# A small mask filled in another step, block 0's weight splits issued in another order, a table held until block 0, and two pads

## The chip, the core and the metric

The kernel runs on one core of a Trainium2 chip. The core has TensorE for matmuls (PE in the profile), VectorE (DVE), ScalarE (ACT), GpSimd (POOL) and SyncE (SP), which issues most DMAs. Each engine serves its own instructions in order and waits for others by semaphores. The metric is the device time of one execution in microseconds (us), as the median of several.

## The reference

Attention, then a mixture of experts on its output, all in float32:

```python
# q, k, v: (8 batches, 8 heads, 576 tokens, 64)
mask_local = (rel >= 0) & (rel < 32)                    # heads 0 to 3
mask_strided = (rel >= 0) & (pos_k % 32 == pos_q % 32)  # heads 4 to 7
attn = softmax(where(mask, q @ k.T / 8, -1e9))          # rows divided by (sum + 1e-9)
x = (attn @ v) with heads side by side                  # (4608 tokens, 512)
logits = x @ w_gate + modality_bias[modality_id]        # 8 experts
e = argmax(logits); g = softmax(logits)[e]
out[token] = g * (relu(x @ w1[e]) @ w2[e])              # w1 512 x 1024, w2 1024 x 512
```

## The kernel before

**Attention** runs in 32 units (classes `Local` and `Strided`), each of which makes scores, a softmax, transposes and values. The order of TensorE is written by hand (`manual_schedule` around the loop over units); that of the other engines comes from the tile framework's scheduler. While units run, generators in `extra` are advanced by `pop`: for each of four pairs of batches (`bp` 0 to 3) they finish the tokens, compute the gate (`route`) and write each token into its expert's region of a buffer `xd` in HBM (`scatter`, indirect DMAs on GpSimd). `going` is a constant 0/1 mask for a scan in `route`.

**Blocks.** The expert layer works on blocks of 256 tokens of one expert, read from `xd`. `PHASES` says when their table is made: after pair 1 that of blocks 0 and 1, after pair 2 that of blocks 2 to 5, after pair 3 that of the rest (first five double blocks, two single ones and a half block). `slots(ph)` computes a table from the counts, with a matmul `ct` and, for blocks 2 to 5, 22 small operations on VectorE. Regions end in rows that nobody wrote; `empty` writes zeros (`in_nul`, 528 KB) over 256 rows of `xd`: once for `xd[0:256]`, and once behind each expert's last row (`blank`).

**One block** is `ffn`. For each of eight parts f of the hidden layer it splits the weights into a high and a low part (`wh` on ScalarE, `wl` on VectorE, in two halves of 512 columns), multiplies (`h`, 12 matmuls in `up`), evicts with relu into `hh` (ScalarE) and `hl` (VectorE), and multiplies again (`o`, 6 matmuls in `down`), two parts later (`LAG`). Its weights come in four tiles j of 1 MB, each for two parts: two tiles `raw`, and the two tiles `lqk` that attention used for queries. `load` fetches those of the next block when a tile is free; `gather` loads tokens (`fx`), `send` splits them into 16-bit halves (`rows`) and transposes them by DMA (`cols`), `split` makes `xh` and `xl`; `turn` does the same for block 0 on TensorE.

**Into block 0.** `early` issues the tokens and the weights of block 0, and the tokens of block 1, during the last units, at the places in `SPOTS`. Each of these is `paced`: it waits until the last matmul ahead of it in the program is done. `split_first` makes the `up` half of f 0 and 1 (`ws`) while attention still runs.

Of the kernel before, what the change touches and what calls it, by code (L numbers as in the profile page):

```python
# [11 lines left out]
F32 = mybir.dt.float32  # L12
# [4 lines left out]
AF = mybir.ActivationFunctionType  # L17
# [3 lines left out]
P = 128  # L21
# [10 lines left out]
PHASES = ((1, 2), (2, 4), (3, 20))  # L32
NDOUBLE, NSINGLE = 5, 2
ROW = DM + 16
# [20 lines left out]
}  # L55
LAG = 2
FIRST, SPLIT, SEND, GATHER, FAR = 1, 4, 6, 7, 6
BIG = -float(2 ** 30)


# [153 lines left out]
def attention_moe(ctx: ExitStack, tc: tile.TileContext, a, out):  # L214
    nc = tc.nc
# [32 lines left out]
    pin = tc.keep_in_program_order  # L248
# [4 lines left out]

    def modality():

        modf = cp.tile([P, 36], F32, name="modf")
        pin(nc.gpsimd.tensor_copy(modf[:], modi))
        nmod = cp.tile([P, 36], F32, name="nmod")
        pin(nc.gpsimd.tensor_scalar(nmod[:], modf[:], -1.0, 1.0, ALU.mult, ALU.add))
        bias0 = ap.tile([P, 36 * E], F32, tag="ls", bufs=1, name="bias0").rearrange("p (t e) -> p t e", e=E)  # L260

        def bc_e(t):
            return t.unsqueeze(2).to_broadcast([P, 36, E])

# [9 lines left out]
    cnt = cp.tile([P, NBP + 1, E], BF16, name="cnt")  # L274
    nc.vector.memset(cnt[:, 0, :], 0.0)
    going = cp.tile([P, E, 9], BF16, name="going")
    nc.vector.memset(going[:], 1.0)
    nc.vector.memset(going[:, :, 0], 0.0)

    written = []  # L280

# [5 lines left out]
    def paced(ins):  # L287

        behind(ins, next(i for i in reversed(nc.cur_bb.bb.instructions) if i.engine == mybir.EngineType.PE).name)
# [23 lines left out]
        tc.add_to_no_dep_group(f"gath{bp}", ins.ins)  # L313

    outs = _Group(tc, "outs")


    ap_cm = tc.tile_pool(name="ap", bufs=1)
# [523 lines left out]

    def empty(rows):
        ins = nc.sync.dma_start(rows, a["nul"])
        for q in range(NBP):
            tc.declare_no_dep(ins.ins, group=f"scat{q}", reason="distinct rows")
            tc.declare_no_dep(ins.ins, group=f"gath{q}", reason="distinct rows")
        tc.declare_no_dep(ins.ins, group="empty", reason="distinct rows")
        tc.add_to_no_dep_group("empty", ins.ins)
        written.append((NBP - 1, ins.ins.name))  # L850

    def first_token(ph, s):
        return nc.values_load(
            tables[ph][0][0:1, s:s + 1], engines=[mybir.EngineType.SP], min_val=0, max_val=E * REG + NT,
            skip_runtime_bounds_check_because="a block's first row of its expert's region")

    def token_rows(dst, rows, bp):
        ins = nc.sync.dma_start(dst, rows)
        if bp < NBP - 1:
            tc.declare_no_dep(ins.ins, group="empty", reason="distinct rows")  # L860
        collected(ins, bp)
        return ins
# [168 lines left out]
            nc.scalar.copy(xh[:, c, q], xs[:, c, :])  # L1031
            nc.vector.tensor_tensor(xl[:, c, q], xs[:, c, :], xh[:, c, q].bitcast(F32), ALU.subtract)  # L1032

    def ffn(fp, n, xh, xl, les, between, load=None):
        os = []
        w = SLOT * len(les)

        def up(f, wh, wl):
            hp = pa(f"h{n}{f}")[:, 0:w]
            k = 0  # L1040
            for c in range(4):
                a1 = slice(P * c, P * c + P)
                for wx, x in ((wh, xh), (wh, xl), (wl, xh)):
                    nc.tensor.matmul(hp, wx[:, a1], x[:, c, :], start=(k == 0), stop=(k == 11))  # L1044
                    k += 1
            if len(les) == 2:
                h2 = ap.tile([P, 2, w], F32R, tag=f"xc{2 + f % 2}", bufs=2, name=f"h2{n}{f}")
                hh, hl = h2[:, 0], h2[:, 1]
            else:
                hh = fp.tile([P, w], F32R, tag="hh", bufs=4, name=f"hh{n}{f}")  # L1050
                hl = fp.tile([P, w], F32R, tag="hl", bufs=4, name=f"hl{n}{f}")
            nc.scalar.activation(hh[:], hp, AF.Relu)  # L1052
            nc.vector.scalar_tensor_tensor(hl[:], hp, 0.0, hh.bitcast(F32), ALU.max, ALU.subtract)  # L1053
            return hh, hl

        def down(f, wh, wl, hh, hl):
            if f == 0:
                os.extend(pa(f"o{n}{h}") for h in range(2 * len(les)))
            for h in range(2 * len(les)):
                m = slice(P * h, P * h + P)  # L1060
                for i, (hx, w) in enumerate(((hh, wh), (hh, wl), (hl, wh))):
                    nc.tensor.matmul(os[h], hx[:, m], w[:, 512:1024],  # L1062
                                     start=(f == 0 and i == 0), stop=(f == 7 and i == 2))

        def finish():
            for h in range(2 * len(les)):
                le = les[h // 2][:, h % 2, :]
                y = fp.tile([P, DM], F32, tag="y", bufs=3, name=f"y{n}{h}")
                nc.scalar.mul(y[:], os[h], le[:, 1:2].bitcast(F32))  # L1069
                outs.add(nc.gpsimd.indirect_dma_start(  # L1070
                    out, IOA(ap=le[:, 0:1], axis=0), y[:], None, bounds_check=NT - 1, oob_is_err=False))

        def down_last(*args):
            down(*args)
            finish()

        for f in range(8):
            raw = raws[f // 2][:, f % 2, :]
            wh = fp.tile([P, 1024], F32R, tag="wh", bufs=5, name=f"wh{n}{f}")
            wl = fp.tile([P, 1024], F32R, tag="wl", bufs=5, name=f"wl{n}{f}")  # L1080
            up_w = ready.pop(f, None)
            for c0 in range(512 if up_w else 0, 1024, 512):
                c = slice(c0, c0 + 512)
                nc.scalar.copy(wh[:, c], raw[:, c])  # L1084
                nc.vector.tensor_tensor(wl[:, c], raw[:, c], wh[:, c].bitcast(F32), ALU.subtract)  # L1085
            if load and f % 2:
                load(f // 2)
            late.append(partial(down_last if f == 7 else down, f, wh, wl, *up(f, *(up_w or (wh, wl)))))
            between(f)
            settle(LAG)  # L1090

# [15 lines left out]

    tables = {}

    def after(bp, xt, xcs):  # L1110
        yield from finish_pair(bp, xt, xcs)
        yield
        for ph, (last_bp, _) in enumerate(PHASES):
            if bp == last_bp:
                yield from slots(ph)
                if ph == 0:
                    yield
                    calm.append(early())

    def early():  # L1120
        for j in range(2):
            n, t, sl = plan[j]
            xt = gathered[j, 0] = pre.tile([P, 2, ROW], F32, tag="fx", name=f"fx{n}0")
            at = first_token(t, sl[0])
            for h in range(2):
                paced(token_rows(xt[:, h, :], xd[bass.ds(at + P * h, P), :], PHASES[t][0]))
                yield
            for part in range(2):
                paced(expert_weights(0, 0, j, part))
                yield  # L1130
        for j in (2, 3):
            paced(expert_weights(0, 0, j))
            yield

    extra, calm = [], []

# [11 lines left out]
    def pop(k):  # L1148
        for _ in range(k):
            while extra and next(extra[0], extra) is extra:  # L1150
                extra.pop(0)
# [20 lines left out]
        return len(plan[k][2]) if k < len(plan) else 1  # L1172

    def gather(k, part=0):
        if k == len(plan):
            gathered[k, 0] = half_tokens()
        if k < len(plan) and part < parts(k):
            n, t, s = plan[k]
            gathered[k, part] = tokens(f"{n}{part}", t, s[part])
# [65 lines left out]
    man.__exit__(None, None, None)  # L1245
    lp_cm.__exit__(None, None, None)

    fp_cm = tc.tile_pool(name="fp", bufs=2, reuse_waits="tile")
    fp = fp_cm.__enter__()
    empty(xd[0:SLOT, :])  # L1250
    while 1 not in tables:
        pop(1)
    gather(2)
    for k, (n, *_) in enumerate(plan):
        def between(f):
            if k == 0 and f == FIRST:
                send(1, 0)
            if f == SPLIT:
                if k + 1 == len(plan):
                    turn(k + 1)  # L1260
                split(k + 1, 0)
            if f == SPLIT - 1 + parts(k + 1):
                split(k + 1, 1)
            if f == SEND:
                send(k + 2, 0)
            if f == GATHER:
                gather(k + 3, 0)
                send(k + 2, 1)
                gather(k + 3, 1)
            pop(POPF[k > 0])  # L1270
            if blanks:
                blanks.pop(0)()

        ffn(fp, n, *turned[k], between, partial(load, k + 1))

    half_ffn(fp, *turned[len(plan)])

# [40 lines left out]
```

## Time and profile before

| | |
|---|---|
| median of 3 runs | 583.71 us (583.25 to 584.79) |
| profiled execution | 579.87 us, its span 577.7, mean granted clock 0.994 |
| TensorE busy | 546.1 us (95% of the span) |
| VectorE, ScalarE, GpSimd busy | 375.9, 313.3, 90.2 us |
| DMA | 137.27 MB, mean 238 GB/s |

In the order of the page: attention takes the first 140 us, block 0 starts at 140, and from there TensorE does the `h` and `o` matmuls of the blocks one after the other. "Idle before <- releaser" in a row says how long the engine had nothing to do ahead of it, and which event ended that.

### The profile page before, as it was taken

What the parts mean: (1) busy time and instruction counts of PE and PEld (TensorE: products, weight loads), DVE (VectorE), ACT (ScalarE), POOL (GpSimd) and SP (SyncE); (2) the same over time, 40 slices, a digit from 0 to 9 for tenths busy, and PEclk for the clock granted to TensorE, in tenths of its full rate; (3) what the DMA queues carried; (4) which work ended last, traced back from release to release, by engine and by line L of the source; (5) the groups of instructions that cost most, each with busy time, mean ns of one, the idle gap of its engine ahead of it and who ended that gap; (6) DMA issues with size and microseconds to landing.
All of it is one profiled execution on the core that took longest, in us unless ns stands there. A gap on an engine that the chain in (4) does not pass through costs nothing.

```text
span 577.7 us, 13484 instructions
## 1 busy us (share of the span) xinstructions
PE 546.1 (95%) x5273; PEld 460.9 (80%) x5273; DVE 375.9 (65%) x942; ACT 313.3 (54%) x651; POOL 90.2 (16%) x106
## 2 busy tenths in 40 slices
PE   6889898898799999999999999999999999999995
PEld 3678677777689999899878888888888888889994
DVE  6887879788586996687765635635734634547541
ACT  3577777767666665566634353344343353356641
POOL 1020321225105311011010020020020020021320
PEclk9999999999899999999999999999999999999998
DMA  8999998979799999999985662572582543555621
GB/s 268 326 321 328 311 301 282 372 257 368 245 367 295 304 387 291 349 322 245 346 231 209 133 251 82 155 276 73 151 233 91 157 172 111 146 201 173 245 94 37
DMA packets 66087, 137.27 MB, mean 238 GB/s; under 512 B 40400, under 2 KB 40784, under 8 KB 58961
## 3 DMA queue, kind: packets, MB, share of 16 engines
q1 hardware_dynamic: 59312, 112.73, 61.3%
q0 software_dynamic: 6416, 23.37, 10.8%
q8 instruction: 43, 0.70, 0.5%
q10 hardware_dynamic: 288, 0.24, 0.1%
q14 instruction: 28, 0.22, 0.1%
HBM read 108.24 MB, written 24.30 MB: 229 GB/s over the span
## 4 chain that ended last, share of the span: by engine, by line
PE 76%; DMA 9%; DVE 6%; issue 4%; ACT 3%; SPq 1%; POOL 0%; POOLq 0%; DVEq 0%; ACTq 0%
PE o L1062 31%; PE h L1044 31%; DMA lqk<-in_w 5%; PE o L437 2%; PE s L389 2%; PE lg L610 1%; DMA cols<-rows 1%; PE oa L533 1%; PE xs L235 1%; DMA raw<-in_w 1%; PE ss L483 1%; PE xl L235 1%; PE t L235 1%; DVE wl L1085 1%; DMA lqk<-in_qkl 1%
## 5 line engine op out<-in xcount | busy, mean ns | idle before, releaser
L1044 PE MATMUL h<-xh,wl 128*128 128x256 f32 (+1 forms) x408 | 133.7, 328 | 0.5 <-DVE wl L1085 0.5
L1044 PE MATMUL h<-xl,wh 128*128 128x256 f32 (+1 forms) x408 | 133.5, 328 | 0.3 <-DVE xl L1032 0.3
L1044 PE MATMUL h<-xh,wh 128*128 128x256 f32 (+1 forms) x408 | 133.5, 328 | 0.0
L1062 PE MATMUL o<-wh,h 128*128 128x512 f32 x320 | 107.0, 396 | 0.0
L1085 DVE TENSOR_TENSOR wl<-lqk,wh 128x512 fp32r<-128x512 f32 x104 | 67.8, 687 | 56.4 <-ACT wh L1084 54.3
L1084 ACT CAST wh<-raw 128x512 fp32r<-128x512 f32 x102 | 58.5, 618 | 65.0 <-PE o L1062 59.7
L1085 DVE TENSOR_TENSOR wl<-raw,wh 128x512 fp32r<-128x512 f32 x102 | 66.4, 686 | 39.3 <-ACT wh L1084 39.2
L1070 POOL DMA_INDIRECT out<-y,le x36 | 40.7, 1130 | 306.3 <-ACT y L1069 299.7
L1084 ACT CAST wh<-lqk 128x512 fp32r<-128x512 f32 x104 | 59.7, 618 | 51.9 <-PE o L1062 49.2
L1044 PEld LDWEIGHTS h<-xl,wh 128*128 128x128 f32 x408 | 77.9, 191 | 10.2 <-DVE xl L1032 0.7
L1044 PEld LDWEIGHTS h<-xh,wh 128*128 128x128 f32 x408 | 77.7, 191 | 9.7
L1044 PEld LDWEIGHTS h<-xh,wl 128*128 128x128 f32 x408 | 77.9, 191 | 8.1 <-DVE wl L1085 0.8
L1062 PEld LDWEIGHTS o<-wh,h 128*128 128x128 f32 x320 | 60.1, 188 | 14.5
L1062 PE MATMUL o<-wl,h 128*128 128x512 f32 x160 | 63.3, 396 | 0.0
L1053 DVE SCALAR_TENSOR_TENSOR h<-h,h 128x512 fp32r<-128x512 f32 x40 | 27.6, 691 | 47.8 <-ACT h L1052 47.8
L1062 PE MATMUL o<-wh,hh 128*128 128x512 f32 x128 | 51.4, 402 | 3.5 <-ACT hh L1052 3.5
L1052 ACT ACTIVATE h<-h 128x512 fp32r<-128x512 f32 x40 | 23.9, 599 | 51.9 <-PE h L1044 51.7
L1062 PE MATMUL o<-wl,hh 128*128 128x512 f32 x128 | 50.6, 395 | 0.0
L1062 PE MATMUL o<-wh,hl 128*128 128x512 f32 x128 | 49.8, 393 | 0.0
L1062 PEld LDWEIGHTS o<-wl,h 128*128 128x128 f32 x160 | 30.0, 188 | 7.1
L1052 ACT ACTIVATE hh<-h 128x256 fp32r<-128x256 f32 x64 | 24.5, 385 | 17.9 <-PE h L1044 17.9
L678 POOL DMA_INDIRECT xd<-xa,posi x20 | 20.7, 1036 | 83.6 <-PE o L1062 30.7
(211 smaller groups left out, 837.8 us busy)
## 6 DMA issues: line engine op xcount, KB each, us to landing
lqk<-in_w SPq DMA_DIRECT2D x26, 1024.0 KB
raw<-in_w SPq DMA_DIRECT2D x24, 1024.0 KB
lqk<-in_qkl SPq DMA_DIRECT2D x32, 296.0 KB
vv<-in_vl SPq DMA_DIRECT2D x32, 292.5 KB
sqk<-in_qks SPq DMA_DIRECT2D x32, 288.0 KB
fx<-xd SPq DMA_DIRECT2D x16, 528.0 KB
vs<-in_vs SPq DMA_DIRECT2D x16, 320.0 KB
xd<-in_nul SPq DMA_DIRECT2D x9, 528.0 KB
```

What stands on the lines that cost most here:

```text
L235: nc.tensor.transpose(dst, src, ident)
L389: nc.tensor.matmul(sp[32 * u:32 * u + 32, 128 * m:128 * m + 128], q[:, i, :], kd[:, :, i:i + 2, :], start=False, stop=True, skip_group_che ...
L437: nc.tensor.matmul(o[64 * jj:64 * jj + 64, k, :], et[:, 2 * (k // 2) + bb, 2 * (k % 2) + jj, :, :].rearrange("p g q -> p (g q)"), vv[:, 4 ...
L483: nc.tensor.matmul(s[32 * u:32 * u + 18, 36 * i:36 * i + 36], qk[:, 32 + r, :], qk[:, r:r + 65:64, :], start=False, stop=True, skip_group_ ...
L678: ins = nc.gpsimd.indirect_dma_start(xd[:], IOA(ap=posi[:, i:i + 1], axis=0), x[:, j, :], None)
L1044: nc.tensor.matmul(hp, wx[:, a1], x[:, c, :], start=(k == 0), stop=(k == 11))
L1052: nc.scalar.activation(hh[:], hp, AF.Relu)
L1053: nc.vector.scalar_tensor_tensor(hl[:], hp, 0.0, hh.bitcast(F32), ALU.max, ALU.subtract)
L1062: nc.tensor.matmul(os[h], hx[:, m], w[:, 512:1024], start=(f == 0 and i == 0), stop=(f == 7 and i == 2))
L1070: outs.add(nc.gpsimd.indirect_dma_start(out, IOA(ap=le[:, 0:1], axis=0), y[:], None, bounds_check=NT - 1, oob_is_err=False))
L1084: nc.scalar.copy(wh[:, c], raw[:, c])
L1085: nc.vector.tensor_tensor(wl[:, c], raw[:, c], wh[:, c].bitcast(F32), ALU.subtract)
```

## The change

- The two memsets of `going` move from VectorE, at the program's start, to GpSimd in `modality`, which is called in unit 9's step.
- `cpad` (4864 bytes a partition) is allocated between the constants and the pool `ap`, `apad` (32 bytes) at the end of `ap`. Neither is read or written.
- `empty` is paced. The write of `xd[0:256]`, which stood first in SP's queue, now stands behind block 0's last weights.
- In block 0 (`first=True`) the splits of f + 1 are issued a step ahead, and from f 2 on a `wh` copy is ordered behind the eviction `hh` of f - 2.
- The table of blocks 2 to 5 waits for `over`, which is set in block 0 at f 1; what waits for the table comes at f 3 (`SECOND`), the tokens of block 2 with it.
- `early` issues in this order: tile 0 of the weights, tokens of block 0, tile 1, tile 2, tokens of block 1, tile 3 (before: tokens of block 0, tile 0, tokens of block 1, tiles 1, 2, 3).
- The half block's tokens are loaded once and not twice.

```diff
+FIRST, SECOND, SPLIT, SEND, GATHER, FAR = 1, 3, 4, 6, 7, 6
+CPAD = 1216
     def modality():
+        pin(nc.gpsimd.memset(going[:], 1.0))
+        pin(nc.gpsimd.memset(going[:, :, 0], 0.0))
...
-    nc.vector.memset(going[:], 1.0)
-    nc.vector.memset(going[:, :, 0], 0.0)
...
+    cp.tile([P, CPAD], F32, name="cpad")
...
     def empty(rows):
         ins = nc.sync.dma_start(rows, a["nul"])
+        paced(ins)
...
+        def split_weights(f):
             raw = raws[f // 2][:, f % 2, :]
...
-                nc.scalar.copy(wh[:, c], raw[:, c])
+                ins = nc.scalar.copy(wh[:, c], raw[:, c])
+                if first and f > 1:
+                    follow(ins, evicted[f - 2])
                 nc.vector.tensor_tensor(wl[:, c], raw[:, c], wh[:, c].bitcast(F32), ALU.subtract)
+            ws[f] = wh, wl, up_w or (wh, wl)
+        for f in range(8):
+            for g in ((f, f + 1) if f == 0 else (f + 1,)) if first else (f,):
+                if g < 8:
+                    split_weights(g)
...
             if bp == last_bp:
+                while ph == 1 and not over:
+                    yield
                 yield from slots(ph)
...
     def early():
...
         for j in range(2):
             for part in range(2):
                 paced(expert_weights(0, 0, j, part))
                 yield
-        for j in (2, 3):
-            paced(expert_weights(0, 0, j))
+            if j == 0:
+                for h in range(2):
+                    paced(half(0, h))
+                    yield
+        paced(expert_weights(0, 0, 2))
+        yield
+        for h in range(2):
+            paced(half(1, h))
             yield
+        paced(expert_weights(0, 0, 3))
+        yield
...
-        if k == len(plan):
+        if k == len(plan) and part == 0:
             gathered[k, 0] = half_tokens()
...
+    ap.tile([P, 8], F32, name="apad")
     empty(xd[0:SLOT, :])
-    while 1 not in tables:
-        pop(1)
-    gather(2)
...
             if k == 0 and f == FIRST:
                 send(1, 0)
+                over.append(True)
+            if k == 0 and f == SECOND:
+                while 1 not in tables:
+                    pop(1)
+                gather(2)
...
-        ffn(fp, n, *turned[k], between, partial(load, k + 1))
+        ffn(fp, n, *turned[k], between, partial(load, k + 1), first=k == 0)
```

ScalarE before, at the start of block 0 (`wh_02` is the high half of block 0's weights for f 2; `xc` are copies for pair 3's tokens):

```order
L1084 CAST wh_00_3138<-raw_2802 128x512
L1084 CAST wh_01_3165<-raw_2802 128x512
L1084 CAST wh_02_3207<-raw_2982 128x512 x2
L1084 CAST wh_03_3250<-raw_2982 128x512 x2
L568 COPY xc_141<-xl_3159 128x512
L1084 CAST wh_04_3289<-lqk_84 128x512 x2
L568 COPY xc_141<-xl_3198 128x512
L568 COPY xc_141<-xl_3204 128x128
L1052 ACTIVATE hh_00_3155<-h_00_3142 128x256
L1052 ACTIVATE hh_01_3186<-h_01_3173 128x256
```

And after:

```order
L1094 CAST wh_00_3095<-raw_2759 128x512
L1094 CAST wh_01_3099<-raw_2759 128x512
L570 COPY xc_140<-xl_3195 128x512
L1060 ACTIVATE hh_00_3116<-h_00_3103 128x256
L1094 CAST wh_02_3120<-raw_2845 128x512 x2
L1060 ACTIVATE hh_01_3143<-h_01_3130 128x256
L1094 CAST wh_03_3201<-raw_2845 128x512 x2
L570 COPY xc_140<-xl_3224 128x512
L570 COPY xc_140<-xl_3230 128x128
L1060 ACTIVATE hh_02_3220<-h_02_3207 128x256
L1094 CAST wh_04_3241<-lqk_83 128x512 x2
```

The evictions `hh` move up between the copies `wh`; `wh_04`, the first that reads a tile `lqk`, moves from ahead of `hh_00` to behind `hh_02`.

VectorE before, in block 0 (`fx_10` and `rows_10` are tokens of block 1):

```order
L1085 TENSOR_TENSOR wl_00_3139<-raw_2802,wh_00_3138 128x512
L1085 TENSOR_TENSOR wl_01_3166<-raw_2802,wh_01_3165 128x512
L1085 TENSOR_TENSOR wl_02_3208<-raw_2982,wh_02_3207 128x512 x2
L1085 TENSOR_TENSOR wl_03_3251<-raw_2982,wh_03_3250 128x512 x2
L1085 TENSOR_TENSOR wl_04_3290<-lqk_84,wh_04_3289 128x512 x2
L1053 SCALAR_TENSOR_TENSOR hl_00_3156<-h_00_3142,hh_00_3155 128x256
L1053 SCALAR_TENSOR_TENSOR hl_01_3187<-h_01_3173,hh_01_3186 128x256
L1000 COPY rows_10_3190<-fx_10_2841 128x2x512 x2
L877 COPY le_10_3196<-fx_10_2841 128x8
L1053 SCALAR_TENSOR_TENSOR hl_02_3227<-h_02_3213,hh_02_3226 128x256
```

And after, from `hl_01` on (`off`, `ei`, `ge`, `tk`, `er`, `own` belong to the table of blocks 2 to 5):

```order
L1061 SCALAR_TENSOR_TENSOR hl_01_3144<-h_01_3130,hh_01_3143 128x256
L1003 COPY rows_10_3147<-fx_10_2972 128x2x512 x2
L880 COPY le_10_3153<-fx_10_2972 128x8
L769 TENSOR_TENSOR off_3166<-used_117,exc_3165 128x8
L787 TENSOR_REDUCE ei_3172<-gi_3170 128x4
L788 TENSOR_TENSOR ge_3171<-cf_sb,exc_3165 128x32
L831 TENSOR_SCALAR tk_3191<-exc_3165 128x8
L1097 TENSOR_TENSOR wl_03_3202<-raw_2845,wh_03_3201 128x512 x2
L806 TENSOR_SCALAR er_3182<-ei_3172 128x4
L789 TENSOR_TENSOR own_3157<-ge_3171,gi_3170 128x32
L832 SCALAR_TENSOR_TENSOR tk_3191<-tk_3191,nb_3162 128x8
L1061 SCALAR_TENSOR_TENSOR hl_02_3221<-h_02_3207,hh_02_3220 128x256
```

`rows_10` moves from behind `wl_04` to ahead of `wl_03`, and operations of the table stand between the splits.

SP after, from block 0's third tile on (names `lqk` hold tiles 2 and 3, `fx_10` the tokens of block 1; ISA rows compute addresses):

```order
L902 DMA lqk_83<-in_w 128x2048
L856 TENSOR_LOAD row_2167
L861 ISA
L861 DMA fx_10_2972<-xd 128x528
L861 ISA
L861 DMA fx_10_2972<-xd 128x528
L902 ISA
L902 DMA lqk_84<-in_w 128x2048
L846 DMA xd<-in_nul 16x8448
L891 TENSOR_LOAD eb_2172
L902 ISA
L902 DMA raw_2759<-in_w 128x2048
```

Tokens of block 1 stand between the third and the fourth tile, the write of zeros behind the fourth, and block 1's first weights follow it, ahead of the transposes of `rows_10`.

## Rows read from the trace of the kernel before

**Rows 1.** Waits of TensorE: for what, us in total, times, longest.
```profile
PE warm L345 <- DVE idle L341: 4.1, 1, 4.1
PE o L1062 <- ACT hh L1052: 3.5, 1, 3.5
...
PE ts L235 <- DVE bl L789: 1.3, 1, 1.3
```

**Rows 2.** Chain that ended last: start us, length us, what ran or landed.
```profile
133.73 14.17 DMA lqk<-in_w
...
151.33 2.56 PE h L1044 x12
156.60 1.43 PE h L1044 x12
```

**Rows 3.** Timeline, start: start us, us, engine, line, operation, [idle before <-releaser].
```profile
0.75 0.61 POOL L337 MEMSET lqk<- 128x608 f32 x1 [0.29 <-POOLq L1310]
...
0.75 0.67 SPq L844 DMA_DIRECT2D xd<-in_nul  x1
...
1.15 0.91 DVE L348 MEMSET et<- 128x1024 f32 x1 [0.16 <-issue]
...
2.35 0.58 POOL L342 MEMSET sqk<- 128x576 f32 x1
...
3.90 0.11 DVE L341 MEMSET idle<- 128x64 uint32 x1
...
8.32 1.08 PE L389 MATMUL s<-lqk 128*32 128x128 f32 x32
```

**Rows 4.** Windows: stretch, length us, busy us of five engines, PEclk, DMA share, GB/s.
```profile
4.00:12.00 8.00, 7.65 (x156) 4.34 (x159) 4.67 (x14) 1.02 (x3) 0.00 (x0) 1.00 0.94 316
125.50:127.50 2.00, 2.00 (x46) 1.74 (x46) 2.00 (x12) 1.43 (x5) 0.00 (x0) 1.00 0.31 75
140.00:147.00 7.00, 6.53 (x59) 6.25 (x55) 4.28 (x8) 4.88 (x9) 5.03 (x5) 1.00 1.03 423
147.00:154.00 7.00, 3.95 (x17) 3.73 (x18) 3.65 (x8) 3.67 (x10) 0.00 (x0) 0.79 0.61 237
154.00:161.00 7.00, 7.00 (x74) 5.39 (x74) 4.74 (x9) 4.97 (x11) 0.00 (x0) 0.97 0.84 240
161.00:168.00 7.00, 7.00 (x49) 6.43 (x48) 5.77 (x16) 5.07 (x12) 0.00 (x0) 1.00 1.02 424
224.00:231.00 7.00, 7.00 (x45) 6.31 (x45) 4.55 (x8) 3.99 (x8) 1.30 (x2) 1.00 1.10 216
237.00:560.00 323.00, 322.19 (x1591) 269.52 (x1590) 187.32 (x322) 155.10 (x283) 34.57 (x32) 1.00 0.61 193
```

**Rows 5.** Timeline, end of attention: SP's token load, TensorE's wait for vs.
```profile
126.03 0.96 SPq L858 DMA_DIRECT2D fx<-xd  x2
...
138.99 1.08 PE L533 MATMUL oa<-eb,vs 126*64 126x126 f32 x16 [1.36 <-DMA vs<-in_vs]
```

**Rows 6.** Timeline, block 0: ScalarE, VectorE and TensorE around the wait.
```profile
147.92 1.14 ACT L1084 CAST wh<-lqk 128x512 fp32r<-128x512 f32 x2 [1.94 <-DMA lqk<-in_w]
148.57 1.29 DVE L1085 TENSOR_TENSOR wl<-lqk,wh 128x512 fp32r<-128x512 f32 x2 [2.27 <-ACT wh L1084]
...
149.60 0.67 ACT L1052 ACTIVATE hh<-h 128x256 fp32r<-128x256 f32 x2
...
150.05 0.50 PE L1062 MATMUL o<-wh,hh 128*128 128x512 f32 x1 [3.52 <-ACT hh L1052]
...
150.70 1.28 DVE L1000 COPY rows<-fx 128x1024 uint16<-128x1024 uint16 x2
...
151.13 0.41 PE L1044 MATMUL h<-xh,wh 128*128 128x256 f32 x1
```

**Rows 7.** Timeline, start of block 4: its tokens on VectorE, TensorE's wait.
```profile
235.87 1.40 DVE L1017 COPY xs<-cols 128x1024 uint16<-128x1024 uint16 x2 [3.98 <-DMA cols<-rows]
...
237.88 0.39 PE L1044 MATMUL h<-xh,wl 128*128 128x256 f32 x1 [0.55 <-DVE wl L1085]
```

More of the change, by code (lines that the diff above doesn't have):

```diff
@@ L56 @@
 LAG = 2
-FIRST, SPLIT, SEND, GATHER, FAR = 1, 4, 6, 7, 6
+FIRST, SECOND, SPLIT, SEND, GATHER, FAR = 1, 3, 4, 6, 7, 6
+CPAD = 1216
 BIG = -float(2 ** 30)
@@ L1032, in split_tokens, with follow, ffn @@
             nc.vector.tensor_tensor(xl[:, c, q], xs[:, c, :], xh[:, c, q].bitcast(F32), ALU.subtract)
-    def ffn(fp, n, xh, xl, les, between, load=None):
-        os = []
+    def follow(ins, other):
+        tc.add_manual_dep(
+            ins.ins, other.ins.name,
+            mybir.DependencyInfo(mybir.DependencyClass.NoSync, mybir.DependencyReason.DATA), reason="order")
+    def ffn(fp, n, xh, xl, les, between, load=None, first=False):
+        os, evicted = [], {}
         w = SLOT * len(les)
@@ L1051, in up @@
                 hl = fp.tile([P, w], F32R, tag="hl", bufs=4, name=f"hl{n}{f}")
-            nc.scalar.activation(hh[:], hp, AF.Relu)
+            evicted[f] = nc.scalar.activation(hh[:], hp, AF.Relu)
             nc.vector.scalar_tensor_tensor(hl[:], hp, 0.0, hh.bitcast(F32), ALU.max, ALU.subtract)
@@ L1075, in down_last @@
             finish()
-        for f in range(8):
+        ws = {}
+        def split_weights(f):
             raw = raws[f // 2][:, f % 2, :]
@@ L1083, in ffn @@
                 c = slice(c0, c0 + 512)
-                nc.scalar.copy(wh[:, c], raw[:, c])
+                ins = nc.scalar.copy(wh[:, c], raw[:, c])
+                if first and f > 1:
+                    follow(ins, evicted[f - 2])
                 nc.vector.tensor_tensor(wl[:, c], raw[:, c], wh[:, c].bitcast(F32), ALU.subtract)
+            ws[f] = wh, wl, up_w or (wh, wl)
[3 more added lines that the diff above has]
+                    split_weights(g)
+            wh, wl, up_w = ws.pop(f)
             if load and f % 2:
                 load(f // 2)
-            late.append(partial(down_last if f == 7 else down, f, wh, wl, *up(f, *(up_w or (wh, wl)))))
+            late.append(partial(down_last if f == 7 else down, f, wh, wl, *up(f, *up_w)))
             between(f)
@@ L1108, in attention_moe @@
     tables = {}
+    over = []
     def after(bp, xt, xcs):
@@ L1120, in early, with half @@
     def early():
-        for j in range(2):
[L1122 to L1127, printed above, removed]
+        firsts = [first_token(plan[j][1], plan[j][2][0]) for j in range(2)]
+        def half(j, h):
+            n, t, _ = plan[j]
+            if h == 0:
+                gathered[j, 0] = pre.tile([P, 2, ROW], F32, tag="fx", name=f"fx{n}0")
+            return token_rows(gathered[j, 0][:, h, :], xd[bass.ds(firsts[j] + P * h, P), :], PHASES[t][0])
+        for j in range(2):
             for part in range(2):
```

## The prediction

> **What bounds the kernel now.** I read four views: TensorE's waits, the chain of what ended last, the timeline around the three places that the change touches, and the windows with the DMA share. TensorE has few waits, and the largest are where the change acts [rows 1]: 4.1 us at the start for the memset of `idle`, 1.3 us at the end of attention for the table of blocks 2 to 5, 3.5 us in block 0 for the eviction `hh`; the 1.4 us for `vs` between them is in [rows 5]. The chain [rows 2] names what stands behind the 3.5: the load of block 0's third weight tile (`lqk`), and the twelve matmuls after it take 2.56 us where twelve later ones take 1.43. Later TensorE runs back to back (busy 322.19 of the 323 us from 237 to 560 [rows 4]). So the time is the sum of matmuls plus these waits, and what is gained before block 1 stays gained unless the DMA stream cannot follow.
>
> Durations come from the profiled execution, 579.87 us (span 577.7); the median of the three timed runs is 583.71, 3.84 more. I sum on 579.87 and carry the 3.84 over.
>
> **1. The start: -1.8 us.** Before, the memset of `idle` starts at 3.90 on VectorE, the warm-up matmuls follow it and the first scores come at 8.32 [rows 3]. Ahead of `idle` stand two `et` memsets of 0.91 us each, which now come later: 2 x 0.91 = 1.8; the smaller ones that leave its front (`going`, `e`) I leave uncounted on the safe side. `idle` so ends near 2.1, the warm-up follows, and the first scores start near 6.5. They also need their load: the write of zeros to `xd` (528 KB), first in SP's queue at 0.75 [rows 3], no longer stands ahead of it. The next limit is the stream of query loads (share 0.94 from 4 to 12 us [rows 4]); it loses the 528 KB ahead of it, about 1.3 us at the 423 GB/s of a later full stretch [rows 4], so a part of the 1.8 could stay there. Bounds: 0 (the loads hold everything) to -2.4 (the small memsets too). I take 1.8, since TensorE, not the loads, was last at 8.32. The two `going` memsets cost nothing on POOL: its memsets at the start end at 2.93, and the mask is first used much later.
>
> In the rows POOL's memset of `lqk` runs from 0.75 to 1.36 and VectorE's `et` from 1.15 to 2.06, side by side, at the same rate per element (0.61 us for 608, 0.91 us for 1024) [rows 3]. The Trainium skill says otherwise for some pairs (SBUF — State Buffer, section SBUF: two separate sides): the port pair that VectorE and GpSimd share is an exclusive lock, and the later one blocks for a whole instruction. [...]
>
> **2. End of attention: -0.8 us.** The 22 small VectorE operations of the table leave this stretch; one of them, `bl`, is what the wait of 1.3 us is put down to [rows 1]. But a little later TensorE waits 1.36 us for `vs` at 138.99 [rows 5], so what comes earlier before it is swallowed there unless `vs` lands earlier. Ahead of `vs` now stands another weight half in place of one token half (512 against 264 KB: +0.25 MB, 0.6 us at 423 GB/s); on the other side SP held the token loads until 126.03, while the stream had a share of only 0.31 from 125.5 to 127.5 [rows 4, 5], and weights, which need no tokens, now fill it: 0.69 x 2 = 1.4 us. So `vs` is 1.4 - 0.6 = 0.8 us earlier. Bounds: +0.6 (the gap isn't filled) to -2.7 (both waits go).
>
> **3. Block 0: -1.6 us.** Before, ScalarE's queue has `wh` f4 (`wh_04`) ahead of `hh_00`; `wh_04` waits for its weights until 147.92, and TensorE's `o` starts at 150.05 after 3.52 us of nothing [rows 6]. After, `hh_00` stands ahead of `wh_02`, and so on alternately. The wait that takes its place is for `wh_02`: after `h_00` ScalarE runs one eviction (two take 0.67, one 0.33) and half a weight copy (1.14 / 2 = 0.57) [rows 6]; together 0.9, if none of it lies beside `h_01`: 3.5 - 0.9 = 2.6. The second half of the copies and the subtractions lie beside the matmuls, which take 1.43 us per f [rows 2].
>
> A new wait on VectorE: `rows_10` waits for `fx1`, which now comes behind the third weight tile, and `wl_03`, the table and `hl_02` queue behind it. `lqk` of the third tile was there at 147.92; 0.5 MB of `fx1` now comes after it and not before it, so the third tile lands earlier and `fx1` at about where the tile was, less the filled gap: 147.9 - 1.4 = 146.5. Two `rows` copies (1.28), the five small operations behind them (some 0.5 by the 0.1 that each holds the queue, an estimate) and half of a `wl` pair (0.65) [rows 6] bring 148.9. TensorE needs `wl_03` in the third matmul of the `h` that started at 151.13 [rows 6] before: 2.6 and the 0.8 of term 2 earlier, and two matmuls later, that is 147.9. So it waits 1.0 there, and term 3 is -2.6 + 1.0 = -1.6. Bounds: 0 (the wait grows to the gain) to -3.5.
>
> **4. The clock: -1.7 us.** Behind the 3.5 us of idle the granted clock is 0.79 from 147 to 154 and 0.97 from 154 to 161 [rows 4]: 0.21 x 7 + 0.03 x 7 = 1.7 us, which is 1.2 GHz for some 3.4 us. Waits of 0.9 and 1.0 are shorter than the 1.3 and 1.4 before it [rows 1, 5], behind which the clock was 1.00 from 140 to 147 [rows 4], so the whole of it comes back. Bounds 0 to -1.7.
>
> **5. Given back at block 4: +0.7 us.** Up to here TensorE is 1.8 + 0.8 + 1.6 + 1.7 = 5.9 us early. From 161 us on the stream is full (share 1.02, 424 GB/s; 1.10 from 224 to 231 [rows 4]), and at 235.87 block 4's tokens come just in time: TensorE waits 0.55 at 237.88 [rows 7]. What the stream can gain: it starts 1.8 + 0.8 = 2.6 earlier; from 147 to 161 it has 0.39 x 7 + 0.16 x 7 = 3.8 us of room, into which block 1's first weights now go (they no longer wait behind the transposes of `cols_10`); and it has the zeros to carry that left the start, +1.4 with their share of the queue. 2.6 + 3.8 - 1.4 = 5.0, so it is 5.9 - 5.0 = 0.9 behind TensorE. The share is under 1 in places after that too, so I take 0.7. Bounds: 0 to +4.7 (no room: 5.9 - 2.6 + 1.4).
>
> That stream rate speaks against a page: the Trainium skill (DMA: Bandwidth & Descriptors, section Where 436 GB/s comes from) lets the HBM side bind at about 358 GB/s for such loads. By it the 161 to 168 stretch could not carry what it did (424, [rows 4]), so the trace disagrees, and the full rate is used above.
>
> **6. Nothing:** the two pads move addresses alone (no row shows a duration that hangs on an address; bounds -1 to +1); the dropped second load of the half block's tokens (264 KB) lies late, where the stream has room; the pacing of the eight zero writes waits on matmuls that are long past.
>
> **The sum:** -1.8 - 0.8 - 1.6 - 1.7 + 0.7 = -5.2: 574.7 profiled, 578.5 as a median.
>
> **Rivals.** A, the forecast: 578.5, its own range 575.5 to 581.5.
>
> B, the stream has no room: block 4 comes 1.2 us earlier (2.6 - 1.4) whatever TensorE does; TensorE waits 4.7 us there and runs its first microseconds at 1.2 GHz, 1.7 more. -1.2 + 1.7 = +0.5: 584.2. For it speaks the share of about 1 from 161 on; against it the 3.8 us of room before that, and that loads ahead of 200 us are released by TensorE's progress.
>
> C, the start gives nothing: VectorE's first memsets wait behind POOL's, which end at 2.93 (2.35 + 0.58) [rows 3], so that `lqk` and `idle` on VectorE end at about 3.6 against 4.0, and the loads hold what is left. The sum without the 1.8: 578.5 + 1.8 = 580.3. Against it: the two engines' memsets side by side.
>
> D, slower: VectorE is held by `rows_10` for `fx1` far longer than the 1.0 of term 3. TensorE idles y = (landing of `fx1`) - 145.5, since 146.5 gives 1.0, and falls to 1.2 GHz behind it, so that term 4 is lost and nothing is given back: -1.8 - 0.8 - 2.6 + y = y - 5.2. It is slower than before from y = 5.2, a landing at 150.7, and tells itself from no change from y = 7; with a landing at 154.5 y is 9: +3.8, 587.5. For it: the slow end of the load of the third tile, and that VectorE serves its queue in order. Against it: `fx1` stands before the fourth tile and the zeros in the queue, and its half tiles are a quarter of a weight tile.
>
> **Numbers.** A 0.58, B 0.16, C 0.13, D 0.13. A measurement of this kernel tells 0.3% from no change, which is 1.75 us: faster is under 581.96, slower above 585.46. A and C are faster (0.71, and a little of B's near side: 0.72); B's middle and D up to y = 7 lie within (0.19); D beyond that and B's far end are slower (0.09). The range 574.5 to 583.8 holds A, C, the near half of B and the first part of D; it leaves out some 0.2.
>
> **What would show it.** The wait for `idle` near 2 us; the wait of `o` for `hh` gone and one under 1 us for `wh` or `wl` in its place; granted clock 1.00 from 147 to 161; `vs` earlier; a wait of some 1 us for `wl_03` behind `rows_10`; at block 4 a wait of `h` for `xs`, `cols` or `wl` of about 1 us, and back to back after it. Wrong if block 4's wait is above 4 us (B), if the first scores stay at 8.3 (C), or if VectorE's wait for `fx` leaves TensorE idle behind `wl_03` for over 3 us (D).

## The result, and the profile after

| | before | after |
|---|---|---|
| median | 583.48 us (4 runs, 580.3 to 584.79) | 576.77 us (4 runs, 573.91 to 577.81) |
| ratio of the medians, 95% interval | | 0.9891 [0.9849, 0.9934] |
| profiled execution, its span, clock | 579.87, 577.7, 0.994 | 577.81, 575.7, 0.987 |

The change makes the kernel 6.7 us faster; 5.2 were forecast. The two profiles differ by only 2.06 us, since the profiled execution of before lies 3.6 us under its median and that of after 1.0 over its own. So the two traces have to be compared by stage. TensorE's first `h` of block 0 is the border: 140.13 us before, 145.71 after. The windows below have the columns of [rows 4]; first four of the kernel before.

```profile
0.00:140.13 140.13, 119.83 (x2986) 97.74 (x2986) 114.10 (x432) 93.72 (x238) 29.31 (x51) 1.00 0.91 310
...
140.13:165.13 25.00, 21.48 (x173) 19.11 (x171) 15.66 (x31) 16.97 (x36) 5.03 (x5) 0.93 0.86 321
...
140.13:577.70 437.57, 426.28 (x2290) 363.16 (x2287) 261.76 (x511) 219.53 (x414) 60.88 (x55) 0.99 0.67 214
...
268.27:519.27 251.00, 250.73 (x1136) 204.83 (x1135) 136.31 (x227) 110.52 (x195) 24.88 (x23) 1.00 0.57 179
```

The first eviction `y` of block 0, before and after, which the reading below also needs:

```profile
177.14 1.38 ACT L1069 ACTIVATE y<-o,le 128x512 f32<-128x512 f32 x2 [0.25 <-PE o L1062]
```

```profile
178.71 1.38 ACT L1077 ACTIVATE y<-o,le 128x512 f32<-128x512 f32 x2 [0.25 <-PE o L1070]
```

The same kind of windows of the kernel after:

```profile
130.00:134.00 4.00, 3.73 (x93) 3.06 (x93) 3.95 (x17) 2.68 (x9) 0.00 (x0) 1.00 0.92 319
...
147.00:154.00 7.00, 6.89 (x50) 6.25 (x50) 6.72 (x23) 5.75 (x15) 5.48 (x6) 1.00 1.01 389
154.00:161.00 7.00, 7.00 (x51) 6.49 (x50) 5.81 (x21) 4.59 (x11) 1.30 (x1) 1.00 1.13 287
...
145.71:170.71 25.00, 24.86 (x197) 21.43 (x195) 20.59 (x58) 18.50 (x41) 7.77 (x7) 1.00 1.05 351
...
237.00:560.00 323.00, 323.00 (x1613) 272.71 (x1613) 186.90 (x321) 156.06 (x286) 35.55 (x34) 1.00 0.61 192
...
0.00:145.71 145.71, 122.94 (x2985) 101.13 (x2986) 113.18 (x406) 93.26 (x236) 27.11 (x52) 0.96 0.88 301
145.71:575.70 429.99, 423.14 (x2291) 361.83 (x2288) 265.44 (x535) 218.95 (x416) 61.88 (x57) 0.99 0.68 217
...
269.31:517.52 248.21, 248.21 (x1136) 204.85 (x1135) 136.06 (x227) 110.18 (x194) 24.69 (x23) 1.00 0.57 178
```

From the first `h` to the end after takes 429.99 us against 437.57: 7.58 less. Of that, 4.44 is TensorE's idle time (437.57 - 426.28 = 11.29 against 6.85), and 3.38 of these lie in the first 25 us of block 0 (3.52 idle before, 0.14 after). The rest, 3.14, is busy time for the same matmuls.

ScalarE's evictions `y` of a block show where the 7.58 lies (the first `y` of block 0 comes at 177.14 before and 178.71 after, that of block 4 at 268.27 and 269.31, the last one of the double blocks at 519.27 and 517.52). Block 0 takes 33.0 us against 37.0, so 4.0 less: the wait, and the granted clock behind it (0.93 before in the first 25 us, 1.00 after). Blocks 1 to 4 take 0.5 less, the end 0.25. The other 2.8 lie in the long stretch from block 4's `y` to the last double block's (block 5 and the five double blocks, the last window of each list above): 251.00 us before, 248.21 after. TensorE has next to no idle time there in either (0.27 and none), the clock is 1.00 in both, and the 1136 matmuls are the same; their mean time is a little shorter after. No term of the forecast has this; the second study below shows which part of the change makes it.

Attention went the other way in this pair of profiles: 145.71 against 140.13 us, at a clock of 0.96 against 1.00. The first study below shows how much of that is the execution and not the code.

TensorE's waits in after (columns of [rows 1]):

```profile
PE ss L485 <- issue: 3.7, 3, 2.1
PE s L391 <- issue: 3.6, 4, 1.7
PE o L439 <- issue: 3.5, 2, 1.9
PE ts L236 <- DVE ec L526: 2.4, 1, 2.4
PE lg L612 <- issue: 2.0, 2, 1.2
PE warm L347 <- DVE idle L343: 1.7, 1, 1.7
```

The 4.1 for `idle` has become 1.7; the waits for `hh`, `bl` and `vs` are gone, and none for `wh` or `wl` stands in their place. From 145 us on no wait of TensorE is listed at all. What is new is the 2.4 for `ec`, and the waits of attention put down to "issue" are larger than before. The timeline of after at two places (the start, block 0):

```profile
0.75 0.60 POOL L339 MEMSET lqk<- 128x608 f32 x1 [0.29 <-POOLq L1346]
...
0.98 0.56 DVE L339 MEMSET lqk<- 128x608 f32 x1
...
1.51 0.11 DVE L343 MEMSET idle<- 128x64 uint32 x1
...
6.15 1.08 PE L391 MATMUL s<-lqk 128*32 128x128 f32 x32 [0.40 <-DMA lqk<-in_qkl]
...
148.78 0.41 ACT L1060 ACTIVATE hh<-h 128x256 fp32r<-128x256 f32 x1
...
149.06 1.17 ACT L1094 CAST wh<-raw 128x512 fp32r<-128x512 f32 x2
...
150.56 0.48 PE L1070 MATMUL o<-wh,hh 128*128 128x512 f32 x1
...
151.54 1.29 DVE L1003 COPY rows<-fx 128x1024 uint16<-128x1024 uint16 x2
```

`idle` now starts at 1.51 and the scores at 6.15, 2.2 us before those of [rows 3]; their row has a short wait for the load, which is the next limit. In block 0 the eviction `hh` stands between the copies of `wh`, and `o` starts without a wait where [rows 6] had 3.52. VectorE's `rows` start with no idle time ahead of them, so the tokens of block 1 (`fx1`) were there. The chain of after names only TensorE's own work through that stretch:

```profile
149.76 0.51 PE h L1052 x2
150.26 0.55 PE xl L236 x5
150.81 1.39 PE o L1070 x6
152.20 1.20 PE h L1052 x10
153.40 0.93 PE o L1070 x4
154.56 0.87 PE xl L236 x8
```

### The profile page after: what moved, and what is told of

The parts are those of the page before. It is cut to its first block, busy times and chain, and to the rows that moved or that the text cites. A ratio compares the mean times of both kernels' runs of the same rounds, so it can differ in the third digit from the quotient of the medians.

```text
span 575.7 us, 13499 instructions
## 1 busy us (share of the span) xinstructions
PE 546.1 (95%) x5273; PEld 463.0 (80%) x5273; DVE 378.6 (66%) x940; ACT 312.2 (54%) x651; POOL 89.0 (15%) x108
## 4 chain that ended last, share of the span: by engine, by line
PE 86%; issue 4%; DVE 4%; ACT 3%; DMA 1%; POOL 0%; SPq 0%; POOLq 0%; DVEq 0%; ACTq 0%
PE h L1052 35%; PE o L1070 35%; PE o L439 2%; PE oa L535 2%; PE s L391 2%; PE lg L612 1%; PE xl L236 1%; PE t L236 1%; PE xs L236 1%; PE ss L485 1%; ACT xc L548 1%; DMA lqk<-in_qkl 1%; PE ts L236 1%; PE s L379 1%; DVE mx L404 0%
## 5 line engine op out<-in xcount | busy, mean ns | idle before, releaser
L1070 PE MATMUL o<-wh,h 128*128 128x512 f32 x320 | 105.8, 392 | 0.0
L1078 POOL DMA_INDIRECT out<-y,le x36 | 39.0, 1083 | 326.8 <-ACT y L1077 320.2
L1061 DVE SCALAR_TENSOR_TENSOR hl<-h,hh 128x256 fp32r<-128x256 f32 x64 | 26.7, 417 | 5.5 <-ACT hh L1060 5.4
```

The costliest lines, as they stand in the source:

```text
L1070: nc.tensor.matmul(os[h], hx[:, m], w[:, 512:1024], start=(f == 0 and i == 0), stop=(f == 7 and i == 2))
L1078: outs.add(nc.gpsimd.indirect_dma_start(out, IOA(ap=le[:, 0:1], axis=0), y[:], None, bounds_check=NT - 1, oob_is_err=False))
```

## The experiments

**One part at a time.** Four kernels took one part of the change each and left the rest as before, on a chip where the kernel before takes 583.27 us, as in the result above. "Blocks" below is the time from the first `h` of block 0 to the end of the profiled execution.

The order of the splits in block 0 alone:

```diff
+                if first and f > 1:
+                    follow(ins, evicted[f - 2])
...
+        for f in range(8):
+            for g in ((f, f + 1) if f == 0 else (f + 1,)) if first else (f,):
+                if g < 8:
+                    split_weights(g)
...
+        ffn(fp, n, *turned[k], between, partial(load, k + 1), first=k == 0)
```

> The kernel before, with the new order of block 0's splits alone. Theory (the terms add): the wait of 3.5 us for hh goes, under 1 us for a split comes in its place, the clock stays up: 4 us faster than before, ratio about 0.993. Rival (the DMA stream has no room): TensorE reaches block 4 earlier and waits there for its tokens, a wait of 3 to 5 us at block 4, ratio 0.998 to 1.000.

Measured: 578.71 us, ratio 0.9931 [0.9894, 0.9968], blocks 431.67. TensorE's wait for `hh` is gone, and 0.6 for `wh` takes its place:

```profile
PE h L1049 <- ACT wh L1091: 0.6, 1, 0.6
```

```profile
148.43:173.43 25.00, 24.43 (x203) 21.82 (x200) 20.02 (x42) 19.17 (x44) 5.47 (x6) 1.00 1.02 370
```

The wait and the lower clock behind it (0.93 in before) are gone in this profile. The window also shows something else: attention's code is unchanged here, and block 0 starts at 148.43, not at 140.13 as in the profile of before. So the 5.58 us by which the result's profiles differ there lie within what single executions of one attention differ by, and are no cost that can be put to the change.

The start alone:

```diff
     def modality():
+        pin(nc.gpsimd.memset(going[:], 1.0))
+        pin(nc.gpsimd.memset(going[:, :, 0], 0.0))
...
-    nc.vector.memset(going[:], 1.0)
-    nc.vector.memset(going[:, :, 0], 0.0)
...
         ins = nc.sync.dma_start(rows, a["nul"])
+        paced(ins)
```

> The kernel before, with the small mask on GpSimd and the write of zeros moved and paced, alone. Theory: first scores near 6.2 us and 1.8 us faster, less at most 1.4 that the zeros cost behind block 0's weights, ratio 0.997 to 0.999. Rival (attention is bound by its loads and the stalls of TensorE's issue, not by its start): the first scores come at 6.2 but the lead is gone by unit 3, ratio 0.999 to 1.002.

Measured: 582.52 us, 0.9989 [0.9955, 1.0022]; blocks 437.84, as before, with a wait for `hh` of 4.4. The wait for `idle` falls to 1.7 and the scores start at 6.53. By the third strided unit VectorE's `sms` stands at 26.02, where before has it at 25.29:

```profile
6.53 1.25 PE L389 MATMUL s<-lqk 128*32 128x128 f32 x32
...
26.02 0.17 DVE L502 TENSOR_SCALAR sms<-sms 128x16 f32<-128x16 f32 x1
...
PE o L1063 <- ACT hh L1053: 4.4, 1, 4.4
```

That looks as if the lead were lost within 20 us, but single executions differ by more than the lead. The same `sms` stands between 25.29 and 29.12 us in the seven profiles of this document with the old start (mean 26.87), and between 25.23 and 26.02 in the seven with the new one (mean 25.72). So on the mean some 1 us of the lead is still there. Nor does the time decide: its interval holds both the forecast's whole 1.8 us (a ratio of 0.9969) and no gain at all.

The held table alone:

```diff
+                while ph == 1 and not over:
+                    yield
...
-    while 1 not in tables:
-        pop(1)
-    gather(2)
...
+            if k == 0 and f == SECOND:
+                while 1 not in tables:
+                    pop(1)
+                gather(2)
```

> The kernel before, with the table of blocks 2 to 5 held until block 0, alone. Theory: the 1.3 us before ts goes but the wait for vs behind it takes it up, and the wait for hh in block 0 stays: 0 to 0.5 us faster, ratio 0.999 to 1.000. Rival: both waits shrink, 1.5 us faster, ratio 0.997.

Measured: 584.82 us, 1.0040 [1.0012, 1.0068], slower by this interval, which neither theory had; the medians differ by 0.3%, and the executions lie among those of the kernel before, so the loss is thin evidence. Blocks 440.94. The wait for `bl` is gone, but a wait for `xh` of 1.2 us stands in the last units in its place, so no gain is seen. The wait for `hh` in block 0 has grown from 3.5 to 4.7; why was not tested.

```profile
PE o L1062 <- ACT hh L1052: 4.7, 1, 4.7
...
PE oa L533 <- ACT xh L987: 1.2, 1, 1.2
```

The load order alone:

```diff
+            if j == 0:
+                for h in range(2):
+                    paced(half(0, h))
+                    yield
+        paced(expert_weights(0, 0, 2))
+        yield
+        for h in range(2):
+            paced(half(1, h))
             yield
+        paced(expert_weights(0, 0, 3))
```

> The kernel before, with the new order of block 0's loads alone. Theory: vs lands 0.8 us earlier, and the third weight tile 1.4 us earlier, so the wait for hh falls from 3.5 to about 2: 2 us faster, ratio 0.9965. Rival: the loads land no earlier, since the queue is full, ratio 1.000.

Measured: 577.74 us, 0.9886 [0.9845, 0.9928]; blocks 432.73. Within the intervals this one part (6 executions) gives as much as the whole change. The wait for `hh` shrinks to 0.9, though the splits stand in the old order, since the third weight tile is there when ScalarE comes to it:

```profile
PE o L1062 <- ACT hh L1052: 0.9, 1, 0.9
```

```profile
148.85 1.15 ACT L1084 CAST wh<-lqk 128x512 fp32r<-128x512 f32 x2
```

So the wait in block 0 is one source of the gain: the two kernels that keep it (4.4 us with the start alone, 4.7 with the held table) gain nothing that can be shown, and the two that remove it gain 0.7 and 1.1%. Two parts of the change reach it from two sides: the load order makes the tile land earlier, the split order moves the eviction ahead of the copy that waits for it. In the profiles the load order alone shortens the blocks by 437.57 - 432.73 = 4.8 us, the split order alone by 437.57 - 431.67 = 5.9, and the whole change by 7.6, less than the 10.7 of the two: for the most part they don't add. What the load order gives at the end of attention, where it also acts, was not told apart.

**Parts taken out of the changed kernel.** The next four ran on a second chip, where the kernel before takes 591.68 us. The changed kernel itself:

> The changed kernel again, beside the three below. Both theories: ratio about 0.989 to the kernel before.

Measured: 591.50 us, 0.9993 [0.9968, 1.0018]. The gain isn't there on this chip. The other three kernels of this study were meant to say which part it hangs on; here each is compared with a change worth nothing in sum. Without the pads:

```diff
-    cp.tile([P, CPAD], F32, name="cpad")
...
-    ap.tile([P, 8], F32, name="apad")
```

> The changed kernel without the two pads. Theory (pads move addresses alone): within 0.3% of the changed kernel, ratio about 0.989. Rival (the pads shift where tiles lie and so how attention's loads run): over 0.5% away from the changed kernel.

Measured: 593.42 us, 1.0025 [1.0000, 1.0049]. This ratio and that of the changed kernel both refer to the kernel before. Set against each other (12 executions each), the kernel without the pads is 2.3 us slower on the mean, with a 95% interval of about 0.9 to 3.6: 0.4%, between theory and rival. The profiles show where. First the long stretch from block 4's `y` to the last double block's, without the pads and then in the changed kernel on the same chip:

```profile
278.56:529.02 250.46, 250.46 (x1136) 204.93 (x1135) 136.13 (x227) 110.18 (x194) 24.88 (x23) 1.00 0.56 176
```

```profile
283.33:531.54 248.21, 248.21 (x1136) 204.87 (x1135) 136.06 (x227) 110.21 (x194) 24.68 (x23) 1.00 0.56 178
```

And the costliest matmul of the double blocks, again first without the pads (count, busy us, mean ns):

```profile
L1069 PE MATMUL o<-wh,h 128*128 128x512 f32 x320 | 107.0, 396 | 0.0
```

```profile
L1070 PE MATMUL o<-wh,h 128*128 128x512 f32 x320 | 105.8, 392 | 0.0
```

TensorE is busy throughout at a granted clock of 1.00 in both, and the same matmuls take 2.25 us longer without the pads. It is so in every profile of this document, on whichever chip: the stretch takes 248.2 us in the five profiles with the pads and 250.5 to 251.2 in the nine without, and the mean of this `o` is 392 ns in the five and 396 in the nine. So the pads, which nothing reads or writes, are worth some 2.3 us. Which of the two it is, and why, no run tells. It also means that of the 7.6 by which the whole change shortens the blocks, some 5.3 are left for block 0 and what follows it, about what the load order or the split order gives alone.

With the old order of the splits:

```diff
-        ffn(fp, n, *turned[k], between, partial(load, k + 1), first=k == 0)
+        ffn(fp, n, *turned[k], between, partial(load, k + 1))
```

> The changed kernel with the old order of block 0's splits. Theory of the forecast (the wait for hh goes by the new order of the splits): the wait of 3 us or more for hh is back, 4 us slower, ratio 0.996. Rival, from the run of the load order alone: the earlier third tile leaves a wait of about 1 us, 0 to 1 us slower, ratio 0.989 to 0.991.

Measured: 589.43 us, 0.9978 [0.9947, 1.0010]. The wait for `hh` is not back; one of 4.2 for `wl` stands in block 0. Set against the changed kernel, neither a loss nor a gain is shown (0.8 us faster on the mean, with an interval of 1.7 to either side). With the table made before block 0:

```diff
-                while ph == 1 and not over:
-                    yield
...
+    while 1 not in tables:
+        pop(1)
+    gather(2)
```

> The changed kernel with the table of blocks 2 to 5 made in attention again. Theory of the forecast (term 2): 0.8 us slower, ratio 0.9905. Rival, from the run of the held table alone, which was 0.4% slower: holding the table costs, so this is 1 to 2.4 us faster than the changed kernel, ratio 0.985 to 0.987.

Measured: 590.06 us, 0.9993 [0.9966, 1.0021]: the wait for `bl` is back at 1.3, and the time is that of the changed kernel, so the loss that the held table alone showed on the first chip isn't seen here. The load order alone, once more:

> The kernel before with the new order of block 0's loads alone, once more. If the chip is one where the kernel before takes 580 to 584 us: theory (the earlier third tile is what the changed kernel gains) says 0.987 to 0.991. If it is one where the kernel before takes 589 to 592: theory (block 0 comes so late there that its weights are there anyway, so that an earlier load gains nothing, but ScalarE's order is the old one, which costs nothing) says 0.998 to 1.001. Rival (the load order itself costs attention time there): over 1.004.

Measured on that second chip: 589.40 us, 0.9984 [0.9953, 1.0015]. What gave 1.1% on the first chip gives nothing that can be measured on this one.

**Why the gain is missing there.** On a third chip, where before takes 589.12, the kernel before was profiled:

> The kernel before, for its profile beside the two below. On the first chip: 4.1 us for idle, 3.5 for hh in block 0, 580 to 584 us. If this is a chip on which the kernel before takes some 591 us: theory (the engines' stalls there are in both kernels, and lay under the wait for the third tile before) says a wait of 4 us or more for hh in block 0 with ScalarE released late; rival (the changed kernel alone has them) says none on ScalarE but the DMA's.

Measured: 589.98 us, one execution. Its block 0 starts at 151.45 us. TensorE has no wait for `hh`, so the theory is refuted, and ScalarE none for a load: when it comes to the third weight tile, at 158.11, the tile has landed. So the wait that the change removes isn't in the kernel before in this profile. That block 0 starts late is not enough for that: on the first chip the start alone had block 0 at 145.26 and waited 4.4 us for `hh` all the same. What TensorE loses in the same 25 us (22.02 busy) are pieces between the transposes `xl`:

```profile
157.59 0.38 PE L235 MATMUL xl<-cf_sb,xa 128*128 128x128 f32 x2 [1.04 <-PE h L1044]
...
158.11 1.14 ACT L1084 CAST wh<-lqk 128x512 fp32r<-128x512 f32 x2
...
159.01 0.38 PE L235 MATMUL xl<-cf_sb,xa 128*128 128x128 f32 x2 [1.04 <-issue]
...
160.46 0.68 PE L235 MATMUL xl<-cf_sb,xb 128*128 128x128 f32 x2 [0.45 <-issue]
```

```profile
151.45:176.45 25.00, 22.02 (x171) 19.07 (x170) 17.78 (x34) 17.76 (x37) 5.76 (x6) 0.93 0.81 294
```

The changed kernel on the second chip starts block 0 at 151.45 too, and there one wait of 6.1 us stands in it, for `wh`:

```profile
PE h L1052 <- ACT wh L1094: 6.1, 1, 6.1
```

```profile
153.29 0.64 PE L236 MATMUL xl<-cf_sb,xa 128*128 128x128 f32 x4
...
153.48 1.14 ACT L1094 CAST wh<-raw 128x512 fp32r<-128x512 f32 x2
158.70 0.58 ACT L570 COPY xc<-xl 128x512 f32<-128x512 f32 x1 [4.07 <-remote]
160.85 0.38 ACT L1060 ACTIVATE hh<-h 128x256 fp32r<-128x256 f32 x1 [1.57 <-remote]
161.13 1.13 ACT L1094 CAST wh<-raw 128x512 fp32r<-128x512 f32 x2
...
161.79 0.58 PE L1052 MATMUL h<-xh,wh 128*128 128x256 f32 x1 [6.09 <-ACT wh L1094]
```

```profile
154.62 4.05 another core or an unknown queue
```

`hh` and the copy `xc` now stand ahead of `wh`, and ScalarE was held at both by an event that the trace doesn't name ("remote"; "another core or an unknown queue" in the chain, of a kernel that runs on one core). It is no weight tile: `wh` behind them starts as soon as ScalarE is free. It is not TensorE's work either: the transposes `xl` that `xc` copies ended at 153.93, and TensorE did nothing from 155.71 to 161.79. Such holds on ScalarE in block 0 are in seven of the eight profiles of these two chips, all but that of the kernel before, and in none of the six of the first. Which engine passes them on to TensorE goes by the order of the queues in most of these profiles: 5.8 to 6.2 us for `wh` on ScalarE in four kernels with the new split order (this one, the one without the pads, the one with the early table, the one with both orders below), 4.2 for `wl` on VectorE with the old split order and the held table, and only pieces of about 1 us with the old order of both (before, and the load order alone). In the first 25 us of block 0 TensorE idles 2.98 us in the kernel before and 3.30 with the load order alone on these chips, and 4.68 to 6.40 in the six profiles with the new split order or the held table. So what the pads give there, the changed kernel loses again in block 0 (6.30 and 4.68 us, against 2.98); that the two cancel is an estimate from single profiles. What the event is stays open; no kernel was run that takes it away.

The changed kernel on the third chip:

> The changed kernel again. Theory: on a chip where the kernel before takes some 583 us, ratio 0.988 to 0.992; where it takes some 591 us, 0.997 to 1.002, as the earlier run there. Rival (the gain does not depend on the chip, the earlier run was chance): about 0.993 on either.

Measured: 589.86 us, 1.0022 [0.9983, 1.0060]; TensorE's waits of `h` in block 0 are 5.2 us in three pieces, put down to "issue". The kernel before with the load order and the split order, that is the two diffs above together, and nothing else:

```diff
+        ffn(fp, n, *turned[k], between, partial(load, k + 1), first=k == 0)
...
+        paced(expert_weights(0, 0, 2))
+        yield
+        for h in range(2):
+            paced(half(1, h))
             yield
+        paced(expert_weights(0, 0, 3))
```

> The kernel before with the new order of block 0's loads and of its splits, without the held table, the moved zeros, the mask and the pads. Theory (both take the same wait, so they do not add): ratio within 0.3% of the load order alone, 0.986 to 0.990 on the first chip, and no slower than the changed kernel. Rival (they add): 0.982.

Measured: 593.35 us, 1.0113 [1.0059, 1.0166] (6 executions), slower than before and than the changed kernel, against the theory: these two parts, each good for 0.7 to 1.1% on the first chip, cost 1.1% together on the third, with a wait of `h` for `wh` of 5.8 us and without the gain of the pads. Neither was run alone on this chip, nor the two together on the first. No version beats the changed kernel clearly: the load order alone is as fast on the first chip and on the second.

## Why the prediction was right, and where it was not

The direction and the size were right, 578.5 against 576.77, and block 0, the largest place of the gain, was named with its mechanism. But that the sum was met so closely is in part luck: one term that was put at nothing gave 2.3 us or more, another came with the wrong sign, and for two no gain is shown.

- **The start (-1.8 forecast).** The rows came as forecast: `idle` at 1.51, the scores 2.2 us earlier. Rival C's mechanism did not occur: POOL's memset of `lqk` from 0.75 to 1.35 and VectorE's from 0.98 to 1.54 ran side by side, 0.60 and 0.56 us for the same size. (The rate per element was not the same, as the prediction reads it: 0.61 us for 608 is 1.00 ns on POOL, 0.91 for 1024 is 0.89 on VectorE.) The Trainium skill (SBUF — State Buffer, section SBUF: two separate sides) has the port pair of these two engines as an exclusive lock for VectorE operations in a 2-port mode or with two inputs from SBUF; a memset has no input, and the trace shows no lock for these. What the term is worth stays open: the start alone measured 0.9989 [0.9955, 1.0022], which holds both the term and rival C's outcome, nothing.
- **The end of attention (-0.8).** Not shown. The gap in the stream ahead of the tokens was filled as forecast: after issues the weights at 130.06, and the share from 130 to 134 is 0.92, where before had 0.31 in the gap [rows 4]. The waits for `bl` and `vs` went, but 2.4 us for `ec` came, and with the held table alone 1.2 for `xh`. The step that is not borne out is that a wait taken out of attention shortens it: in these profiles another one came.
- **Block 0 (-1.6) and the clock (-1.7).** The place and the mechanism were right: 4.0 us less by the rows of `y`, where the two terms have 3.3. The forecast let 0.9 for `wh` and 1.0 for `wl` take the place of the 3.5. In after neither came (0.14 us idle in 25). The estimate had left out work that TensorE has in between: the transposes `xl` of pair 3's tokens stand between `h` and `o` in the chain (0.55 and 0.87 us), which is the likely cover of the copies; no run took them away. And `fx1` was there when VectorE came to `rows`, so that rival D did not occur. The splits alone, without the earlier tile, did show 0.6 of the 0.9. The clock of 1.00 from 147 to 161 is as forecast.
- **The cause of that gain.** The forecast took the removed wait from the split order and let the load order only fill a gap. The runs show that either removes it: the load order alone leaves 0.9 of the 3.5, the split order alone 0.6 for `wh`.
- **Given back at block 4 (+0.7).** Did not come; the 0.55 of before [rows 7] went too (TensorE is busy 323.00 of 323). Rival B's time, 584.2, is refuted by the measured one. Its condition was not met in the profile, though: TensorE came to block 4 no earlier than before (the first `y` of block 3 at 247.57 against 245.71), since block 0 had started 5.6 later.
- **Nothing (pads and the rest).** For the pads this was wrong: they shorten the long stretch of double blocks by some 2.3 us (248.2 against 250.5 to 251.2). The trace of before has no row for it, as the prediction says, and the term's bounds of -1 to +1 were too narrow. The half block's single load was in no run by itself.

Behind the first `h` of block 0 the forecast had -1.6 - 1.7 + 0.7 = -2.6, and the two profiles differ by -7.58: -4.0 in block 0, -0.5 in blocks 1 to 4, -2.8 in block 5 and the double blocks, -0.25 at the end. The 5.0 more stand against the 2.6 forecast ahead of block 0, for which no gain is shown. And all of this holds for the first chip alone: the forecast had no rival in which the wait for `hh` isn't there.

## What to carry to other kernels

Of a wait removed at the start or within a stage full of loads no gain could be shown here, so count it only where the engine itself sets the pace from there on (here from block 0). When a removed wait has two possible causes, such as queue order and landing time, price each alone, since either may take it all. Do not put a change that only moves addresses at nothing: compare the mean time of each matmul form, and set two variants against each other instead of asking whether their intervals to a third kernel overlap. A gain of 1% that hangs on when a load lands should be measured on more than one chip: here it was 1.1% on one and nothing on two others.

## What the runs showed of the hardware

- **Chips differ.** The same kernel before took 583 us on one chip and 589 to 592 on two others; in the profiles block 0 starts at 146.93 (without the pads) to 151.45 us there and at 140.13 to 148.43 on the first. These ranges overlap; what sets the chips apart in block 0 are the holds that the trace doesn't name, which only the two others show.
- **Executions differ.** With the same attention code the first `h` of block 0 came at 140.13 (before) and 148.43 (split order alone) on one chip. Single profiles can't be subtracted. A stage in which TensorE has no waits can: the stretch of block 5 and the double blocks took 248.20 or 248.21 us in all five profiles with the pads.
- **Where tiles lie has a price.** Two pads that nothing reads or writes took the mean of the double blocks' `o` from 396 to 392 ns, at a granted clock of 1.00 in both. The cause is open.
- **Stalls of TensorE put down to "issue"** sum to 9.0 us in attention of before and 14.5 in that of after (its rows above, 3.7 + 3.6 + 3.5 + 2.0, and 0.9 and 0.8 more), up to 2.1 us at a time in these two, beside a granted clock over attention of 1.00 and of 0.96. No run was made to tell what they are.
